# Batch 0 taken in the order q, k, v by halves of the heads, and k and v of two batches laid six tokens to a partition

## The chip, the cores and the metric

The kernel runs on one core of one Trainium2 chip. The metric is device time in microseconds for one launch. In the profile the engines are called PE (TensorE, matrix multiplies), PEld (TensorE's weight loads, which run beside its multiplies), DVE (VectorE), ACT (ScalarE), POOL (GpSimd) and SP (SyncE). SP and POOL issue most of the DMAs here, POOL those that turn f32 in HBM into bf16 in on-chip memory. Each engine works through its own list of instructions in order, and waits at an instruction until what that needs is there.

## The reference: what is computed

Two parts follow each other. The first is a linear attention over 8 batches of 8 heads, 576 tokens and 64 features: q and k are clipped at zero and multiplied by the cosine and by the sine of a position angle, which gives 128 features; then k is summed against v over the tokens.

```
q_p = phi(q, cos_w, sin_w)          # max(x, 0) times cos, beside max(x, 0) times sin: 128 features
k_p = phi(k, cos_w, sin_w)
kv  = einsum('bhsf,bhsd->bhfd', k_p, v)
z   = sum(k_p, axis=2)
num = einsum('bhsf,bhfd->bhsd', q_p, kv)
den = einsum('bhsf,bhf->bhs', q_p, z)[..., None] + 1e-06
x   = (num / den), all heads of a token side by side: 4608 tokens of 512
```

The second part is a feed-forward layer over the 4608 tokens: h = x @ w_in (512 to 2048), g = h * sigmoid(1.702 h), out = g @ w_out (2048 to 512).

## The kernel before

**Layout.** A batch of q, k or v has 576 tokens. The first 512 lie four to a partition on 128 partitions (`load_main`), so that token 4p + c is chunk c of partition p; the last 64 are a tail of their own, one to a partition on 64 partitions (`load_tail`), and are chunk 4. `kp` holds k after the clipping and the two multiplications, five chunks by 8 heads by 128 features; `vt` holds v in bf16 with a 65th column of ones, so that one multiplication gives both kv and z. `qn` is q after the same treatment, and `qT` is `qn` turned so that features lie on the partitions.

**The steps of one batch.** `prep` makes a chunk of `kp` or `qn` (two operations, cosine and sine, L179 on DVE or L177 on ACT). `prep_v` casts a chunk of v into `vt` (L182). `unit_kv` multiplies `kp` with `vt`, 8 heads by five chunks (L213), and copies the result to `kvs` (L217). `turn_q` turns a chunk of q by a DMA transpose (L189), `turn_q_at` by eight matmuls with the identity and a DVE copy (L195, L196). `unit_num` multiplies a chunk of `qT` with `kvs` (L233), and DVE divides (L239 to L241) into `xb`. `turn_x` or `turn_x_at` turns `xb` into `xT` (L206, or L201 and L203).

**The feed-forward layer** goes over nine blocks of 512 tokens. A block has 32 slots: 16 `mm1` (four matmuls of L249 and an ACT activation, L254), then 16 groups of four matmuls of `mm2` (L289). Nothing is scheduled by a planner: the order of every engine's instructions is the order in which the program writes them. The attention of batch i + 1 is written into the slots of block i by `at(slot, function)`: the function comes right after that slot's matmuls. In block 0 the numbers are k0 = 14 (preparing batch 1's q and turning it), k1 = 25 (`unit_kv`), and 26 to 29 for the `unit_num`s.

**The front** is batch 0's own attention, ahead of block 0. PE starts with 34 matmuls on zeros (L68). k comes first, in f32, by one load on SP (L109), then its tail and v's tail on SP; q and v come through POOL. ACT and DVE prepare k together, then DVE prepares q chunk by chunk, `turn_q0` turns each chunk (L331, copied by L332), and v is cast by halves of the heads. kv of heads 0 to 3 is `kv_lo`, of heads 4 to 7 `kv_hi`. `num0(n, p)` multiplies half n of the heads with the pair p of chunks (L338) and lets ACT make the denominator (L342); `product0` divides on DVE (L348, L349); `turn_x0` turns the result (L355, L357). The first three groups of `mm1` are written out by hand in parts (`mm1_first`, L361), as far as `xT` is there. The tail of batch 0's q is prepared last and turned by a DMA transpose into `qT_tail`; `unit_num(0, 4)` uses it in slot 7 of block 0.

**Buffers.** `mm` has four PSUM buffers of one bank, `at` two of two banks: a new use waits for the readers of the use four (or two) before. `qn` has one buffer, q, k and v of later batches two each. POOL has at most eight DMAs under way: the ninth waits until the first has landed.

Of the kernel before, what the change touches and what calls it, by code (L numbers as in the profile page):

```python
# [9 lines left out]
F32 = mybir.dt.float32  # L10
# [11 lines left out]
def kernel(  # L22
# [27 lines left out]

    def rows(c):
        return 128 if c < 4 else 64

    warm = const.tile([128, TB], BF16)
    nc.vector.memset(warm, 0.0)  # L57

    def mm_tile():
        return ps.tile([128, TB], F32, name="mm", bufs=4)  # L60
# [11 lines left out]
    SRC = {"q": q, "k": k, "v": v}  # L72

    def load_main(b, n, h0=0, h1=H, on=nc.gpsimd):
        if h0 == 0:
            state[b][n] = two.tile([128, 2048], BF16, name=n)
        on.dma_start(out=state[b][n][:, 256 * h0:256 * h1].rearrange("p (h e) -> p h e", h=h1 - h0),  # L77
                     in_=SRC[n][b, h0:h1, 0:512, :].rearrange("h (p c) d -> p h (c d)", c=4))
# [23 lines left out]
    def load_w_out(g):  # L102
        nc.gpsimd.dma_start(out=w_out_sb[:, ts(g, 4), :], in_=wout_r[:, ts(g, 4), :])

    pos_i = const.tile([128, NC], I32)
    id_i = const.tile([128, 128], I32)
# [12 lines left out]
    load_w_in(0, 0, 2)  # L119
# [19 lines left out]
    kp = one.tile([128, NC, H, 2 * D], BF16, name="kp")  # L139
    vt = one.tile([128, NC, H, VW], BF16, name="vt")  # L140
    qT = one.tile([128, H, NC * 128], BF16, name="qT")
    nc.vector.memset(kp[64:128, 4], 0.0)
    nc.vector.memset(vt[64:128, 4], 0.0)
    nc.vector.memset(vt[:, 0:4, :, D:D + 1], 1.0)
    nc.vector.memset(vt[0:64, 4, :, D:D + 1], 1.0)
    qT_tail = one.tile([128, H, 128], BF16, name="qT_tail")
    nc.vector.memset(qT[:, :, S:NC * 128], 0.0)
    nc.vector.memset(qT_tail[:, :, 64:128], 0.0)
    pos_f = const.tile([128, NC], F32)
    nc.vector.tensor_copy(pos_f, pos_i)  # L150
    ident = const.tile([128, 128], BF16)
    nc.vector.tensor_scalar(ident, id_i, 0.0, None, op0=EQ)
    sinw = const.tile([128, NC], F32)
    cosw = const.tile([128, NC], F32)
    nc.scalar.activation(sinw, pos_f, AF.Sin, scale=scale)
    nc.scalar.activation(cosw, pos_f, AF.Sin, scale=-scale, bias=halfpi)
    gelu0 = const.tile([128, 1], F32)
    nc.scalar.activation(gelu0, halfpi, AF.Gelu_apprx_sigmoid)

# [1 line left out]


    def part(b, n, c, h0, h1):
        if c == 4:
            return state[b][n, 4].rearrange("p (h d) -> p h d", d=D)[:, h0:h1]
        return state[b][n].rearrange("p (h c d) -> p c h d", c=4, d=D)[:, c, h0:h1]

    def prep_new(b):
        state[b]["qn"] = one.tile([128, NC, H, 2 * D], BF16, name="qn")
# [1 line left out]

    def prep(b, n, c, h0=0, h1=H, on=(nc.vector, nc.vector)):
        o = state[b]["qn"] if n == "q" else kp
        for cs, w in enumerate((cosw, sinw)):
            oc, i, wc = o[:rows(c), c, h0:h1, cs * D:cs * D + D], part(b, n, c, h0, h1), w[:rows(c), c:c + 1]
            if on[cs] is nc.scalar:
                nc.scalar.activation(oc, i, AF.Relu, scale=wc)  # L177
            else:
                nc.vector.tensor_scalar(oc, i, 0.0, wc, op0=MAX, op1=MUL)  # L179

    def prep_v(b, c, h0=0, h1=H):
        nc.vector.tensor_copy(vt[:rows(c), c, h0:h1, 0:D], part(b, "v", c, h0, h1))  # L182

    def q_slot(b, c):

# [22 lines left out]


    def kv_half(b, n, kv):  # L210
        for h in range(4 * n, 4 * n + 4):
            for c in range(NC):
                nc.tensor.matmul(kv[:, ds(h % 4 * (D + 1), D + 1)], kp[:, c, h, :], vt[:, c, h, 0:D + 1],  # L213
                                 start=(c == 0), stop=(c == NC - 1))

    def kvs_half(b, n, kv, copy=nc.vector.tensor_copy):
        copy(state[b]["kvs"][:, n, :, 0:D + 1], kv[:, 0:4 * (D + 1)].rearrange("p (h e) -> p h e", h=4))  # L217

    def kvs_new(b):
        state[b]["kvs"] = two.tile([128, 2, 4, VW], BF16, name="kvs")  # L220
# [102 lines left out]

    prep_new(0)
    s0 = state[0]
    dens = {}

    def turn_q0(c, copy):
        t = mm_tile().bitcast(BF16).rearrange("p (h t) -> p h t", h=H)
        for h in range(H):  # L330
            nc.tensor.transpose(t[:, h], s0["qn"][:, c, h, :], ident)  # L331
        copy(qT[:, :, ts(c, 128)], t)  # L332
# [12 lines left out]
    def product0(n, p):  # L345
        nm4, den = dens[n, p]
        inv = two.tile([128, 2, 4], F32, name="inv")
        nc.vector.reciprocal(inv, den)  # L348
        nc.vector.tensor_tensor(s0["xb"][:, 2 * p:2 * p + 2, 4 * n:4 * n + 4, :], nm4[:, :, :, 0:D],  # L349
                                inv.unsqueeze(3).to_broadcast([128, 2, 4, D]), op=MUL)  # L350
# [12 lines left out]

    AC, VE = nc.scalar, nc.vector
    kvs_new(0)
    warmup(34)
    for c in range(4):
        prep(0, "k", c, on=(VE, AC))
    prep(0, "k", 4)
    for c in range(2):  # L370
        prep(0, "q", c)
        turn_q0(c, AC.copy)
    prep_v(0, 4)
    for c in range(4):
        prep_v(0, c, 0, 4)
    kv_lo = mm_tile()
    kv_half(0, 0, kv_lo)
    kvs_half(0, 0, kv_lo, AC.copy)
    num0(0, 0)
    for c in (2, 3):  # L380
        prep(0, "q", c)
    for c in range(4):
        prep_v(0, c, 4, 8)
    turn_q0(2, AC.copy)
    product0(0, 0)
    turn_q0(3, VE.tensor_copy)
    kv_hi = mm_tile()
    kv_half(0, 1, kv_hi)
    kvs_half(0, 1, kv_hi, AC.copy)
    num0(0, 1)  # L390
    product0(0, 1)
    tp = mm_tile().bitcast(BF16).rearrange("p (q s j t) -> p q s j t", q=2, s=2, j=2)
    first = [mm_tile() for _ in range(3)]
    turn_x0(0, 0)
    num0(1, 0)
    product0(1, 0)
    turn_x0(0, 1)
    num0(1, 1)
    product0(1, 1)
    turn_x0(1, 0)  # L400
    for fc in range(3):
        mm1_first(fc, (0, 1), 0, TB)
    turn_x0(1, 1)
    for p in range(2):
        for fc in range(3):
# [87 lines left out]
```

## Time and profile before

| | us |
|---|---|
| median of 4 runs (lowest to highest) | 300.14 (299.38 to 301.56) |
| the profiled execution | 299.71 |
| span of its instructions | 297.6 |
| PE busy | 286.5 (96%) |
| DVE, ACT, POOL busy | 107.4, 120.6, 92.5 |
| first matmul of L249 in the main loop | 22.46 |
| start of block 1 | 57.0 |
| last matmuls (L313) | 289.76 to 293.26 |

The span is that of the profiled execution, from the first instruction to the last. Its own time is 2.1 us longer, and lies within the range of the runs. A row of the profile has the line of the kernel, the engine, the operation, what it writes and reads, and how often; in the timeline and the chain the first two numbers are start and length in us from the start of the span.

### The profile page before, as it was taken

The numbers are of one execution on the slowest core, as the hardware profiler recorded it, in microseconds if no ns is written. First come the engines' busy times: TensorE is split into PE (matmuls) and PEld (weight loads), VectorE is DVE, ScalarE is ACT, GpSimd is POOL, SyncE is SP. The second block draws the span as 40 slices with busy tenths as digits, with TensorE's granted clock in tenths as the row PEclk, the third lists the DMA queues.
The fourth block names the chain that finished last, engine by engine and source line by source line (L and its number), as shares of the span: only waits on it lengthen the run. The fifth ranks groups of instructions, "written<-read, shape, count | busy, mean of one in ns | idle before, by whom it ended". The sixth has DMA issues, their size and how long they took to land.

```text
span 297.6 us, 5050 instructions
## 1 busy us (share of the span) xinstructions
PE 286.5 (96%) x1956; PEld 144.6 (49%) x1956; DVE 107.4 (36%) x349; ACT 120.6 (41%) x205; POOL 92.5 (31%) x113
## 2 busy tenths in 40 slices
PE   8877999999999999999999999999999999999994
PEld 3563455545544554455445544554455444444443
DVE  3860376781590158115811481148214200000000
ACT  5555600664127412651165116511651176136410
POOL 8442130440269025800690159004401200120021
PEclk9999999999999999999999999999999999999999
DMA  8999999999979955997699789946804500021033
GB/s 193 195 204 194 184 193 195 200 153 151 203 156 182 184 100 128 192 163 136 134 176 178 121 144 192 193 89 134 176 0 64 124 35 2 36 79 27 2 71 71
DMA packets 89847, 39.84 MB, mean 134 GB/s; under 512 B 58656, under 2 KB 87584, under 8 KB 89824
## 3 DMA queue, kind: packets, MB, share of 16 engines
q0 software_dynamic: 41312, 26.68, 59.3%
q1 hardware_dynamic: 48352, 12.72, 24.1%
q8 instruction: 15, 0.25, 0.3%
q10 hardware_dynamic: 160, 0.13, 0.2%
q14 instruction: 8, 0.07, 0.1%
HBM read 36.70 MB, written 9.44 MB: 155 GB/s over the span
## 4 chain that ended last, share of the span: by engine, by line
PE 86%; DVE 6%; DMA 6%; issue 1%; ACT 0%; DVEq 0%; POOLq 0%
PE mm L249 39%; PE mm L289 38%; PE at L233 3%; DMA q<-in_q_dram 3%; PE at L213 3%; DMA qT_tail<-qn 3%; PE mm L313 1%; DVE kp L179 1%; DVE qn L179 1%; DVE xb L349 1%; DVE vt L182 1%; PE at L195 1%; DVE xb L241 1%; DVE qT L196 0%; ACT den L342 0%
## 5 line engine op out<-in xcount | busy, mean ns | idle before, releaser
L289 PE MATMUL mm<-w_out_sb,g 128*128 128x512 bf16 x560 | 129.0, 379 | 0.0
L249 PE MATMUL mm<-xT,w_in_sb 128*128 128x512 bf16 (+1 forms) x568 | 124.6, 377 | 0.0
L254 ACT ACTIVATE g<-mm 128x512 bf16<-128x512 f32 x144 | 85.6, 597 | 48.1 <-PE mm L249 47.5
L301 POOL DMA_DIRECT2D out_dram<-ysb x54 | 50.6, 941 | 173.7 <-ACT ysb L299 173.0
L249 PEld LDWEIGHTS <-w_in_sb 128*128 128x128 bf16 x568 | 54.7, 98 | 64.1 <-issue 0.2
L289 PEld LDWEIGHTS <-g 128*128 128x128 bf16 x560 | 52.1, 98 | 56.5
L299 ACT COPY ysb<-mm 128x512 f32<-128x512 f32 x34 | 19.9, 586 | 112.7 <-PE mm L289 109.4
L217 DVE CAST kvs<-at 128x260 bf16<-128x260 f32 x14 | 5.4, 426 | 56.3 <-PE at L213 56.3
L241 DVE TENSOR_TENSOR xb<-at,inv 128x512 bf16<-128x512 f32 (+1 forms) x36 | 24.8, 689 | 1.2
L239 DVE TENSOR_SCALAR den<-at 128x8 f32<-128x8 f32 (+1 forms) x36 | 5.9, 164 | 53.0 <-PE at L233 53.0
L318 DVE COPY ysb<-mm 128x256 f32<-128x256 f32 x1 | 0.4, 425 | 59.4 <-PE mm L313 59.4
L233 PEld LDWEIGHTS <-qT 128*128 128x128 bf16 x280 | 13.4, 98 | 8.4 <-DVE xb L241 0.6
L233 PE MATMUL at<-kvs,qT 128*128 128x65 bf16 x280 | 14.6, 194 | 0.3
L179 DVE TENSOR_SCALAR kp<-k,cosw 128x512 bf16<-128x512 bf16 (+1 forms) x32 | 12.2, 389 | 3.5 <-DMA k<-in_k_dram 3.5
L213 PEld LDWEIGHTS <-kp 128*128 128x128 bf16 x320 | 11.1, 97 | 2.6 <-ACT qT L332 0.4
L179 DVE TENSOR_SCALAR qn<-q,sinw 128x512 bf16<-128x512 bf16 x32 | 11.5, 361 | 0.0
L179 DVE TENSOR_SCALAR qn<-q,cosw 128x512 bf16<-128x512 bf16 x32 | 11.0, 345 | 0.6 <-DMA q<-in_q_dram 0.6
L68 PE MATMUL mm<-warm 128*128 128x512 bf16 x34 | 9.4, 446 | 1.2 <-DVE warm L57 1.2
L213 PE MATMUL at<-vt,kp 128*128 128x65 bf16 x280 | 10.1, 193 | 0.2
L179 DVE TENSOR_SCALAR kp<-k,sinw 128x512 bf16<-128x512 bf16 x28 | 9.5, 340 | 0.0
L77 POOL DMA_DIRECT2D v<-in_v_dram x9 | 7.9, 883 | 2.0 <-DMA w_out_sb<-in_moe_w_out_dram 2.0
L77 POOL DMA_DIRECT2D q<-in_q_dram x8 | 7.5, 936 | 3.4 <-DMA w_in_sb<-in_moe_w_in_dram 2.0
(67 smaller groups left out, 119.4 us busy)
## 6 DMA issues: line engine op xcount, KB each, us to landing
out_dram<-ysb POOLq DMA_DIRECT2D x38, 128.0 KB, 3.0
q<-in_q_dram POOLq DMA_DIRECT2D x8, 512.0 KB, 9.3
out_dram<-ysb POOLq DMA_DIRECT2D x16, 256.0 KB, 2.7
k<-in_k_dram POOLq DMA_DIRECT2D x7, 512.0 KB, 11.2
v<-in_v_dram POOLq DMA_DIRECT2D x7, 512.0 KB, 12.7
w_out_sb<-in_moe_w_out_dram POOLq DMA_DIRECT2D x4, 512.0 KB, 24.7
w_in_sb<-in_moe_w_in_dram POOLq DMA_DIRECT2D x3, 512.0 KB, 13.8
k<-in_k_dram SPq DMA_DIRECT2D x1, 1024.0 KB, 5.8
```

The source lines that it names most:

```text
L68: nc.tensor.matmul(wps, warm[:, 0:128], warm, start=True, stop=True)
L77: on.dma_start(out=state[b][n][:, 256 * h0:256 * h1].rearrange("p (h e) -> p h e", h=h1 - h0), in_=SRC[n][b, h0:h1, 0:512, :].rearrange("h ...
L179: nc.vector.tensor_scalar(oc, i, 0.0, wc, op0=MAX, op1=MUL)
L213: nc.tensor.matmul(kv[:, ds(h % 4 * (D + 1), D + 1)], kp[:, c, h, :], vt[:, c, h, 0:D + 1], start=(c == 0), stop=(c == NC - 1))
L233: nc.tensor.matmul(nm[:, h // 4, ds(h % 4 * (D + 1), D + 1)], q_slot(b, c)[:, h, :], state[b]["kvs"][:, h // 4, h % 4, 0:D + 1], start=Tru ...
L239: nc.vector.tensor_scalar(den[:r], nm4[:, :, :, D], 1e-6, None, op0=ADD)
L241: nc.vector.tensor_tensor(state[b]["xb"][:r, c].rearrange("p (n h) d -> p n h d", n=2), nm4[:, :, :, 0:D], inv[:r].unsqueeze(3).to_broadca ...
L249: nc.tensor.matmul(hps[:, c0:c1], w_in_sb[:, kc, ds(fc * 128, 128)], xT[:, kc, ds(i * TB + c0, c1 - c0)], start=(kc == 0), stop=(kc == KC ...
L254: nc.scalar.activation(g, hps, AF.Gelu_apprx_sigmoid)
L289: nc.tensor.matmul(yps, gT[fc][:, ds(t * 128, 128)], w_out_sb[:, fc, :], start=(fc == 0), stop=(fc == FC - 1))
L299: nc.scalar.copy(ysb, cur[t])
L301: nc.gpsimd.dma_start(out=out[row:row + (n - 1) * step + 1:step, :], in_=ysb[p0:p0 + n, :])
```

## The change

Batch 0 is taken in the order q, k, v:

- q of batch 0 is what SP loads in f32, in two halves of four heads (`q0`); k goes through POOL in two halves of the heads, ahead of v. The tails of k and v of batch 0 are no longer loaded by themselves.
- k and v of batches 0 and 1 have six tokens to a partition on 96 partitions (`wide`), all 576 tokens in one load, with position tables of their own (`pos6_i`, `cos6`, `sin6`). `kp` and `vt` have six chunks; `unit_kv` of batch 1 goes over six chunks of 96 rows instead of five. Of batch 1 SP loads only q's tail. From batch 2 on the old layout holds, so that the 64 unused rows of chunk 4 of `kp` and `vt` are zeroed in slot 2 of block 1.
- v of batch 0 is not copied to `vt`: `kv0` multiplies `kp` with the loaded tile itself. Each matmul has 128 moving columns, 64 of v and 64 ones from a strip behind it (48 * D to 49 * D).
- `turn_q0(n, p)` turns two chunks of half the heads. Three of the four are done ahead of k. `num0` has its denominator made by DVE, and `product0` is merged into it. 30 warm-up matmuls instead of 34.
- In block 0, `unit_num(0, 4)` goes from slot 7 to 13, k0 from 14 to 11 with all five chunks of q in one slot and their turns in slots 14 to 18, k of batch 1 into slot 18, k1 from 25 to 23, the `unit_num`s to slots 24 to 27.

```diff
     def load_main(b, n, h0=0, h1=H, on=nc.gpsimd):
+        t = 6 if wide(b, n) else 4
+        np_ = 96 if wide(b, n) else 128
...
-    state[0]["k"] = k0 = one.tile([128, 2048], F32, name="k0")
-    nc.sync.dma_start(out=k0.rearrange("p (h e) -> p h e", h=H),
-                      in_=k[0, :, 0:512, :].rearrange("h (p c) d -> p h (c d)", c=4))
-    load_tail(0, "k", nc.sync)
-    load_tail(0, "v", nc.sync)
-    load_main(0, "q")
+    state[0]["q"] = q0 = one.tile([128, 2048], F32, name="q0")
+    for n in range(2):
+        nc.sync.dma_start(out=q0[:, ts(n, 1024)].rearrange("p (h e) -> p h e", h=4),
+                          in_=q[0, 4 * n:4 * n + 4, 0:512, :].rearrange("h (p c) d -> p h (c d)", c=4))
     nc.gpsimd.iota(pos_i[:, 0:4], pattern=[[1, 4]], base=0, channel_multiplier=4)
     nc.gpsimd.iota(pos_i[:, 4:5], pattern=[[1, 1]], base=512, channel_multiplier=1)
+    nc.gpsimd.iota(pos6_i, pattern=[[1, 6]], base=0, channel_multiplier=6)
+    load_main(0, "k", 0, 4)
     nc.gpsimd.iota(id_i, pattern=[[1, 128]], base=0, channel_multiplier=-1)
+    load_main(0, "k", 4, 8)
     load_main(0, "v", 0, 4)
     load_main(0, "v", 4, 8)
...
     def kv_half(b, n, kv):
+        r, last = (96, 5) if b < 2 else (128, 4)
         for h in range(4 * n, 4 * n + 4):
-            for c in range(NC):
-                nc.tensor.matmul(kv[:, ds(h % 4 * (D + 1), D + 1)], kp[:, c, h, :], vt[:, c, h, 0:D + 1],
-                                 start=(c == 0), stop=(c == NC - 1))
+            for c in range(last + 1):
+                nc.tensor.matmul(kv[:, ds(h % 4 * (D + 1), D + 1)], kp[:r, c, h, :], vt[:r, c, h, 0:D + 1],
+                                 start=(c == 0), stop=(c == last))
...
+    def turn_q0(n, p, copy):
+        t = mm_tile().bitcast(BF16).rearrange("p (h s t) -> p h s t", h=4, s=2)
+        for h in range(4):
+            for s in range(2):
+                nc.tensor.transpose(t[:, h, s], s0["qn"][:, 2 * p + s, 4 * n + h, :], ident)
+        copy(qT[:, 4 * n:4 * n + 4, ds(256 * p, 256)].rearrange("p h (s t) -> p h s t", s=2), t)
+
+    def kv0(n):
+
+        kv = mm_tile()
+        v3 = s0["v"][:96].rearrange("p (j d) -> p j d", d=D)
+        for h in range(4):
+            for c in range(6):
+                j = (4 * n + h) * 6 + c
+                nc.tensor.matmul(kv[:, ts(h, 128)].rearrange("p (j d) -> p j d", j=2), kp[:96, c, 4 * n + h, :],
+                                 v3[:, j:49:48 - j, :], start=(c == 0), stop=(c == 5))
+        kvs_half(0, n, kv, nc.scalar.copy, 128)
...
-        nc.scalar.activation(den, nm4[:, :, :, D], AF.Identity, bias=eps)
-        dens[n, p] = nm4, den
-
-    def product0(n, p):
-        nm4, den = dens[n, p]
         inv = two.tile([128, 2, 4], F32, name="inv")
+        nc.vector.tensor_scalar(den, nm4[:, :, :, D], 1e-6, None, op0=ADD)
         nc.vector.reciprocal(inv, den)
...
-    warmup(34)
...
+    warmup(30)
+
+    def prep_q0(n, p):
+        for c in (2 * p, 2 * p + 1):
+            prep(0, "q", c, 4 * n, 4 * n + 4)
+
+    for n, p in ((0, 0), (0, 1), (1, 0)):
+        prep_q0(n, p)
+        turn_q0(n, p, AC.copy)
+    for c in range(6):
+        prep(0, "k", c, 0, 4)
+    prep_q0(1, 1)
+    for c in range(6):
+        prep(0, "k", c, 4, 8, on=(VE, AC))
+    kv0(0)
+    turn_q0(1, 1, AC.copy)
     num0(0, 0)
...
     num0(0, 1)
-    product0(0, 1)
+    kv0(1)
     tp = mm_tile().bitcast(BF16).rearrange("p (q s j t) -> p q s j t", q=2, s=2, j=2)
     first = [mm_tile() for _ in range(3)]
     turn_x0(0, 0)
     num0(1, 0)
-    product0(1, 0)
     turn_x0(0, 1)
     num0(1, 1)
-    product0(1, 1)
-    turn_x0(1, 0)
     for fc in range(3):
         mm1_first(fc, (0, 1), 0, TB)
+        if fc == 0:
+            turn_x0(1, 0)
     turn_x0(1, 1)
...
-    for n in "kvq":
-        load_tail(1, n, nc.sync)
+    load_tail(1, "q", nc.sync)
...
             if i == 0:
-                at(7, unit_num, 0, 4)
-                at(7, turn_x, 0, 4)
-            k0, k1, ks = (14, 25, (26, 27, 28, 29)) if i == 0 else (0, 12, (17, 19, 21, 23, 25))
+                at(13, unit_num, 0, 4)
+                at(13, turn_x, 0, 4)
+            k0, k1, ks = (11, 23, (24, 25, 26, 27)) if i == 0 else (0, 12, (17, 19, 21, 23, 25))
             at(k0, prep_new, b)
+            if i == 1:
+
+                at(2, nc.vector.memset, kp[64:128, 4], 0.0)
+                at(2, nc.vector.memset, vt[64:128, 4], 0.0)
             for c in range(NC):
-                at(22 if i == 0 and c == 4 else k0, prep, b, "q", c)
+                at(k0, prep, b, "q", c)
                 if i == 0:
-                    at(23 if c == 4 else k0 + 2 + c, turn_q_at, b, c)
+                    at(k0 + 3 + c, turn_q_at, b, c)
                 else:
                     at(k0 + c, turn_q, b, c)
-                at(k1 - 4 + c // 2, prep, b, "k", c)
+            for c in range(6 if b < 2 else NC):
+                at(18 if i == 0 else k1 - 4 + c // 2, prep, b, "k", c)
                 at(k1 - 1, prep_v, b, c)
             at(k1, unit_kv, b)
```

More of the change, by code (lines that the diff above doesn't have):

```diff
@@ L54, in rows, with wide, krows @@
         return 128 if c < 4 else 64
+    def wide(b, n):
+        return b < 2 and n != "q"
+    def krows(b, c):
+        return 96 if b < 2 else rows(c)
     warm = const.tile([128, TB], BF16)
@@ L74, in load_main @@
     def load_main(b, n, h0=0, h1=H, on=nc.gpsimd):
+        t = 6 if wide(b, n) else 4
+        np_ = 96 if wide(b, n) else 128
         if h0 == 0:
-            state[b][n] = two.tile([128, 2048], BF16, name=n)
-        on.dma_start(out=state[b][n][:, 256 * h0:256 * h1].rearrange("p (h e) -> p h e", h=h1 - h0),
-                     in_=SRC[n][b, h0:h1, 0:512, :].rearrange("h (p c) d -> p h (c d)", c=4))
+            state[b][n] = two.tile([128, 2048 if n == "q" else 49 * D], BF16, name=n)
+        on.dma_start(out=state[b][n][:np_, t * D * h0:t * D * h1].rearrange("p (h e) -> p h e", h=h1 - h0),
+                     in_=SRC[n][b, h0:h1, 0:np_ * t, :].rearrange("h (p c) d -> p h (c d)", c=t))
     def load_tail(b, n, on=nc.gpsimd):
@@ L105 @@
     pos_i = const.tile([128, NC], I32)
+    pos6_i = const.tile([128, 6], I32)
     id_i = const.tile([128, 128], I32)
-    state[0]["k"] = k0 = one.tile([128, 2048], F32, name="k0")
-    nc.sync.dma_start(out=k0.rearrange("p (h e) -> p h e", h=H),
-                      in_=k[0, :, 0:512, :].rearrange("h (p c) d -> p h (c d)", c=4))
-    load_tail(0, "k", nc.sync)
-    load_tail(0, "v", nc.sync)
-    load_main(0, "q")
+    state[0]["q"] = q0 = one.tile([128, 2048], F32, name="q0")
+    for n in range(2):
+        nc.sync.dma_start(out=q0[:, ts(n, 1024)].rearrange("p (h e) -> p h e", h=4),
+                          in_=q[0, 4 * n:4 * n + 4, 0:512, :].rearrange("h (p c) d -> p h (c d)", c=4))
     nc.gpsimd.iota(pos_i[:, 0:4], pattern=[[1, 4]], base=0, channel_multiplier=4)
     nc.gpsimd.iota(pos_i[:, 4:5], pattern=[[1, 1]], base=512, channel_multiplier=1)
+    nc.gpsimd.iota(pos6_i, pattern=[[1, 6]], base=0, channel_multiplier=6)
+    load_main(0, "k", 0, 4)
     nc.gpsimd.iota(id_i, pattern=[[1, 128]], base=0, channel_multiplier=-1)
+    load_main(0, "k", 4, 8)
     load_main(0, "v", 0, 4)
@@ L138, with table @@
     nc.vector.memset(eps, 1e-6)
-    kp = one.tile([128, NC, H, 2 * D], BF16, name="kp")
-    vt = one.tile([128, NC, H, VW], BF16, name="vt")
+    pos_f = const.tile([128, NC], F32)
+    nc.vector.tensor_copy(pos_f, pos_i)
+    pos6_f = const.tile([128, 6], F32)
+    nc.vector.tensor_copy(pos6_f, pos6_i)
+    ident = const.tile([128, 128], BF16)
+    nc.vector.tensor_scalar(ident, id_i, 0.0, None, op0=EQ)
+    kp = one.tile([128, 6, H, 2 * D], BF16, name="kp")
+    vt = one.tile([128, 6, H, VW], BF16, name="vt")
     qT = one.tile([128, H, NC * 128], BF16, name="qT")
[L142 to L145, printed above, removed]
     qT_tail = one.tile([128, H, 128], BF16, name="qT_tail")
+    nc.vector.memset(state[0]["v"][:, 48 * D:49 * D], 1.0)
+    nc.vector.memset(vt[:, :, :, D:D + 1], 1.0)
     nc.vector.memset(qT[:, :, S:NC * 128], 0.0)
     nc.vector.memset(qT_tail[:, :, 64:128], 0.0)
[L149 to L156, printed above, removed]
+    def table(name, shape, pos, bias, sign):
+        t = const.tile(shape, F32, name=name)
+        nc.scalar.activation(t, pos, AF.Sin, scale=sign * scale, bias=bias)
+        return t
+    cosw = table("cosw", [128, NC], pos_f, halfpi, -1.0)
+    sinw = table("sinw", [128, NC], pos_f, 0.0, 1.0)
+    cos6 = table("cos6", [128, 6], pos6_f, halfpi, -1.0)
+    sin6 = table("sin6", [128, 6], pos6_f, 0.0, 1.0)
     gelu0 = const.tile([128, 1], F32)
@@ L163, in part @@
     def part(b, n, c, h0, h1):
+        if wide(b, n):
+            return state[b][n][:96, 0:48 * D].rearrange("p (h c d) -> p c h d", c=6, d=D)[:, c, h0:h1]
         if c == 4:
             return state[b][n, 4].rearrange("p (h d) -> p h d", d=D)[:, h0:h1]
-        return state[b][n].rearrange("p (h c d) -> p c h d", c=4, d=D)[:, c, h0:h1]
+        return state[b][n][:, 0:32 * D].rearrange("p (h c d) -> p c h d", c=4, d=D)[:, c, h0:h1]
     def prep_new(b):
@@ L173, in prep @@
         o = state[b]["qn"] if n == "q" else kp
-        for cs, w in enumerate((cosw, sinw)):
-            oc, i, wc = o[:rows(c), c, h0:h1, cs * D:cs * D + D], part(b, n, c, h0, h1), w[:rows(c), c:c + 1]
+        r = rows(c) if n == "q" else krows(b, c)
+        for cs, w in enumerate((cos6, sin6) if wide(b, n) else (cosw, sinw)):
+            oc, i, wc = o[:r, c, h0:h1, cs * D:cs * D + D], part(b, n, c, h0, h1), w[:r, c:c + 1]
             if on[cs] is nc.scalar:
@@ L181, in prep_v @@
     def prep_v(b, c, h0=0, h1=H):
-        nc.vector.tensor_copy(vt[:rows(c), c, h0:h1, 0:D], part(b, "v", c, h0, h1))
+        nc.vector.tensor_copy(vt[:krows(b, c), c, h0:h1, 0:D], part(b, "v", c, h0, h1))
     def q_slot(b, c):
@@ L210, in kv_half, with kvs_half @@
     def kv_half(b, n, kv):
+        r, last = (96, 5) if b < 2 else (128, 4)
         for h in range(4 * n, 4 * n + 4):
-            for c in range(NC):
-                nc.tensor.matmul(kv[:, ds(h % 4 * (D + 1), D + 1)], kp[:, c, h, :], vt[:, c, h, 0:D + 1],
-                                 start=(c == 0), stop=(c == NC - 1))
-    def kvs_half(b, n, kv, copy=nc.vector.tensor_copy):
-        copy(state[b]["kvs"][:, n, :, 0:D + 1], kv[:, 0:4 * (D + 1)].rearrange("p (h e) -> p h e", h=4))
+            for c in range(last + 1):
+                nc.tensor.matmul(kv[:, ds(h % 4 * (D + 1), D + 1)], kp[:r, c, h, :], vt[:r, c, h, 0:D + 1],
+                                 start=(c == 0), stop=(c == last))
+    def kvs_half(b, n, kv, copy=nc.vector.tensor_copy, w=D + 1):
+        copy(state[b]["kvs"][:, n, :, 0:D + 1],
+             kv[:, 0:4 * w].rearrange("p (h e) -> p h e", h=4)[:, :, 0:D + 1])
     def kvs_new(b):
@@ L325 @@
     s0 = state[0]
[L326 to L332, printed above, removed]
+    nums = {}
+    def turn_q0(n, p, copy):
[13 more added lines that the diff above has]
+        kvs_half(0, n, kv, nc.scalar.copy, 128)
     def num0(n, p):
@@ L365 @@
     kvs_new(0)
-    warmup(34)
[L367 to L378, printed above, removed]
-    num0(0, 0)
[L380 to L389, printed above, removed]
+    warmup(30)
[12 more added lines that the diff above has]
+    turn_q0(1, 1, AC.copy)
+    num0(0, 0)
     num0(0, 1)
-    product0(0, 1)
+    kv0(1)
     tp = mm_tile().bitcast(BF16).rearrange("p (q s j t) -> p q s j t", q=2, s=2, j=2)
```

## The prediction

> **What bounds the kernel now.** I read the engine totals first, then the stretches of busy time, the chain of work that ended last, PE's waits in the first block, and then the timeline of the first 57 us.
>
> ```profile
> PE 286.5 (96%) x1956; PEld 144.6 (49%) x1956; DVE 107.4 (36%) x349; ACT 120.6 (41%) x205; POOL 92.5 (31%) x113
> ...
> 57.00:265.00 208.00, 208.00 (x1388) 102.55 (x1386) 76.61 (x256) 83.27 (x140) 68.63 (x74) 1.00 0.82 132
> ```
>
> The second line is a stretch, with PE's busy time first: from 57.0 us, where block 1 starts, PE never stops. What the change does can therefore show only in when block 1 starts. That has two parts: the front (batch 0's attention, until the first main-loop matmul of L249 at 22.46 us) and block 0 (from there to 57.0).
>
> ```profile
> 13.64 0.39 ACT kvs L217
> ...
> 19.70 0.69 DVE xb L349
> 20.39 0.66 DVE qn L179 x2
> 21.04 0.02 issue
> 21.06 7.73 DMA qT_tail<-qn
> 28.79 0.05 issue
> 28.84 0.43 PE at L233 x8
> 29.26 6.91 PE mm L249 x32
> ...
> 45.18 0.42 PE at L195 x8
> ...
> 46.83 1.15 DVE vt L182 x5
> 47.98 0.04 issue
> 48.02 1.24 PE at L213 x36
> ```
>
> This is the chain, with start and length. PE is full but for stalls: unit_num(0,4) waits for the DMA transpose of q's tail, then the last turn of batch 1's q waits for DVE, then kv of batch 1 waits for the copies of v. PE's waits give the first its size:
>
> ```profile
> PE at L233 <- DMA qT_tail<-qn: 1.9, 1, 1.9
> PE at L195 <- DVE qn L179: 0.3, 1, 0.3
> ```
>
> In the timeline the kv matmuls begin at 47.25 and go on in earnest at 48.02: 0.77 more. The L233 groups of chunks 2 and 3 begin at 52.75 and 54.40, each 0.31 after PE came free. Stalls of block 0: 1.89 + 0.31 + 0.77 + 0.62 = 3.6 us.
>
> **The front, step by step.** Before, its last part is kvs_hi (ACT, ends 16.40), then four rounds of num0 and product0 on DVE, the last L361 matmuls, and L249 at 22.46. The new order makes ACT the engine that is late. The rows:
>
> ```profile
> 1.19 9.39 PE L68 MATMUL mm<-warm 128*128 128x512 bf16 x34 [1.19 <-DVE warm L57]
> 6.60 2.56 ACT L177 ACTIVATE kp<-k,sinw 128x512 bf16<-128x512 f32 x4 [1.71 <-DMA k<-in_k_dram]
> 11.68 1.93 ACT L332 COPY qT<-mm 128x1024 bf16<-128x1024 bf16 x2 [2.52 <-PE mm L331]
> ```
>
> - Warm-up: from 5.0 us its matmuls start 0.215 apart; four fewer end it 0.86 earlier, near 9.7. The transposes of q follow in order; eight take 0.45, so ACT's first copy starts at 10.2.
> - q must be there by then. The 1 MB of k on SP landed at 0.74 + 5.8 = 6.5; the same bytes are now q's two halves, estimated at 5.0 and 6.4. Twelve DVE multiplies of 256 f32 elements at about 0.3 (half of 0.585, the spacing of four of 512 in 2.34) end near 8.7. POOL's two added halves of k, one added iota and the iotas now ahead of the loads delay its first load by about 0.4, but its queue moved only 0.03 MB before 6 us while SP's load ran, so nothing is lost. At 0.2 MB/us after that, k lands by halves near 8.3 and 9.7, v near 11.2 and 12.7.
> - ACT, in order: three copies of 1024 columns (0.92 apart, 1.01 alone: 2.85), until 13.05. Then six multiplies of k's high half by the sine, 256 columns each. [...] The row has 0.707 us for 512 columns and 0.617 from one to the next; scaled by the columns alone, six would take 1.85. [...] ACT reaches kvs of the low half at 15.4 (0.38): 15.75.
> - kv0 of the low half is 24 matmuls of 128 moving columns, 0.056 each as in the transposes: 1.35. Even if it waits for all of v it ends near 14.1, and the turn of q's last quarter follows: hidden behind ACT. So the omitted casts of v (1.5 us of DVE) and the memsets buy nothing here; DVE is free from 12.8.
> - num0(0,0): 0.45 on PE. Then DVE makes den (0.21), inv (0.23) and the product (0.69), 1.13 a round by L239 to L241's spacing; taking den over from ACT costs DVE 0.2 and saves a hop. kv0 of the high half sits behind two num0s on PE (16.5 to 17.85), its kvs copy ends at 18.3, and round three starts at 18.75, 0.25 after round two ended. Round four ends at 21.0, against 20.4 before.
> - Transpose (0.25), ACT copy (0.6), last six matmuls (0.65), with 0.3 between: L249 starts at 22.8. **Front: +0.35.** Bounds: -0.2 with ACT's six by columns, +1.0 if v's high half is 2 us later than estimated.
>
> **Block 0.**
> - unit_num(0,4) moves from slot 7 to 13, which begins eleven matmul groups of 0.863 (29.26 6.91 x32: 0.216 each) after 22.8, at 32.3. The tail's transpose starts near 21.7 and with 7.73 lands at 29.45. **-1.89**, hidden by six more groups of mm1; cover left 2.9.
> - Now all of batch 1's q is prepared at slot 11, ahead of that unit's den on DVE. The new qn has one buffer, so it waits for the same transpose: 29.45, eight operations of 0.26: 31.55. The fifth chunk needs the tail of q, loaded by SP right behind the transpose. kt and vt of batch 1 are gone from that queue:
>
> ```profile
> kt<-in_k_dram SPq DMA_DIRECT2D x1, 128.0 KB, 8.9
> qt<-in_q_dram SPq DMA_DIRECT2D x1, 128.0 KB, 13.8
> ...
> q0 software_dynamic: 237, 0.12, 87.8%
> q1 hardware_dynamic: 237, 0.06, 45.8%
> ```
>
> The first two lines are issue to landing: 22.41 + 8.9 = 31.3 and 23.73 + 13.8 = 37.5. The last two are packets and MB in the microsecond from 31: the queues take turns packet by packet, and SP's 512 packets of 256 bytes take 2.1 us at 240 per us, 3.2 at 160. So q's tail lands at 31.6 to 32.7; I take 32.0, since kt in the same place took 2.5. DVE ends it at 32.8, and the tail unit's three operations at 33.9, before the second turn wants its PSUM buffer at 34.8. No stall; the earlier 0.31 goes.
> - k and v of batch 1: six chunks where there were five. Turns end on PE at 39.1, the last copy on DVE at 39.55; twelve multiplies at 0.26 end at 42.8, six casts (0.20 apart) at 44.05. PE reaches kv at 43.4 and loses 0.5 where it lost 0.77: **-0.27**. Eight more matmuls (1.21 / 40 each): **+0.24**. The product stalls (0.62) stay.
> - Transfers: w_out's second quarter landed at 15.79 + 24.3 = 40.1 (wanted at 39.9), v of batch 1 at 16.54 + 26.2 = 42.7 (wanted at 42.8), w_out's third quarter at 45.3 (wanted at 45.3). All would be just in time even unmoved. Without kt and vt POOL's queue runs at 0.2 and not 0.13 MB/us for about 5 us (0.35 MB, 1.8 us), less 0.13 MB of tails that it now carries (0.7): about 1 us earlier. **0.**
> - The two memsets of kp and vt in block 1 (0.76) lie in DVE's idle time before slot 8: 0; without cover they'd cost that.
>
> Sum: +0.35 - 1.89 - 0.31 - 0.27 + 0.24 = -1.9. The span goes from 297.6 to 295.7, the profiled execution from 299.71 to 297.8, and the median from 300.14 to **298.2**.
>
> **Rivals.**
> - *The gain is eaten in the front* (0.14; about 299.5). PE is loaded unevenly from 11 to 19 us. [...] Warm-up shows both speeds (0.43 and 0.215 apart), and the stall of 1.9 at 27 us left no slow matmul. [...] ACT or DVE slower by 1.3 us ends in the same place.
> - *q's tail holds DVE* (0.12; slower). It is queued on DVE in front of the tail unit and of every turn's copy, which free PE's buffers. Past about 32.9 each us of lateness costs PE one; at 34.8 the gain is gone. At the old 37.5, DVE is done with the tail unit at 39.4, PE waits from 34.8, and 4.6 - 1.9 gives 302.8. Against it: two loads of 512 packets left that queue.
> - *96 partitions load slower than 128* (0.08). If four such loads (2.36 MB, 12 us at 0.2 MB/us) ran at three quarters, v lands 4 us later less 1, its casts end at 47.1, kv stalls 3.7 for 0.5: 301.3. No row shows such a load.
> - *ACT's short operations scale, and DVE's rounds close up* (0.12): 297.2.
>
> **How the numbers follow.** Measurement tells about 0.5% (1.5 us) from no change. The sum as it stands has 0.54, with its own range 297.3 to 299.1, of which 0.46 lies under 298.6. Faster: 0.46 + 0.12 = 0.58; same: 0.08 + 0.14 = 0.22; slower: 0.12 + 0.08 = 0.20. The range runs from 296.6, the front at -0.2 with DVE's 0.5 at kv gone too and 0.6 for the rounding of a dozen terms, to 301.5, past the slow-load case; the late tail's far end stays outside.
>
> **What would show it.** The kvs copy of the low half near 15.4 on ACT, right behind six short multiplies; L249 near 22.8; no wait of L233 for qT_tail; L213 in block 0 near 43.9 behind DVE; block 1 near 55.1; no gap after. Wrong if PE stands at the first turns of batch 1's q while DVE waits for a DMA, if kv waits for v's load, or if matmuls in L361 start 0.43 apart.

## The result

The changed kernel takes 297.13 us (median of 30 runs, 296.37 to 301.91), the kernel before 299.84 (49 runs, 299.06 to 302.12). The ratio is 0.9915, with a 95% interval of 0.9899 to 0.9931: 0.85% faster, 2.5 us (2.7 between the medians). The forecast was 298.2, 1.9 us faster.

In some executions of either kernel PE's mean clock is lower: 0.982 to 0.994 in 17 of 42 of the changed kernel, with a median of 299.08 where the other 25 have 296.86 (the profiled one, 299.08 with a span of 297.3, is of the 17, at 0.993), and 0.989 to 0.996 in 26 of 81 of the kernel before, of which 16 took 301.25 or more where the other 55 have a median of 299.64.

First the chain of work that ended last, of the changed kernel, with start and length in us. The lines of before have moved: L238 is the old L217 (kvs), L271 the old L249, L255 the old L233, L215 the old L195, L234 the old L213.

```profile
10.78 2.84 ACT qT L355 x3
13.62 2.37 ACT kp L197 x6
15.99 0.27 ACT kvs L238
16.26 0.04 issue
16.31 0.97 PE at L372 x16
17.28 2.57 PE mm L364 x24
...
25.25 9.50 PE mm L271 x44
34.74 0.25 PE at L255 x8
35.00 0.86 PE mm L271 x4
35.86 0.45 PE at L215 x8
...
46.31 1.46 PE at L234 x43
```

Two things are to be seen. In block 0 the tail unit (L255) follows its slot's matmuls without a gap, and so do the first turns (L215); no DMA stands on the chain any more where it had 7.7 us. In the front ACT's six sines stand before kvs, as foretold, and PE waits behind them. The 24 matmuls of L364 take 2.57 us, though (2.75 by the timeline, where the low half's 24, at 11.79, take 1.50 at a clock of 1.00).

PE's row in the timeline has the length of that wait in brackets; the stretches of the same profile have the granted clock as the third number from the end (after PE, PEld, DVE, ACT and POOL):

```profile
16.31 0.97 PE L372 MATMUL at<-kvs,qT 128*128 128x65 bf16 x16 [2.57 <-ACT kvs L238]
```

```profile
10.00:15.00 5.00, 3.58 (x58) 3.20 (x57) 4.16 (x18) 4.22 (x7) 3.17 (x4) 1.00 1.32 192
15.00:20.00 5.00, 3.69 (x44) 3.69 (x44) 2.03 (x6) 2.28 (x6) 2.73 (x4) 0.66 1.27 206
20.00:25.00 5.00, 4.30 (x49) 2.99 (x47) 2.67 (x8) 2.65 (x6) 0.80 (x1) 1.00 1.34 202
```

PE waited 2.57 us, until 16.31, and the clock was 0.66 in the stretch from 15 to 20. By the timeline the main loop then starts at 25.08 us and block 1 at 57.07, no earlier than before (22.46 and 56.85). The run of the changed kernel below has a profile at full clock.

### The profile page after: what moved, and what is told of

Same layout as the page of the kernel before. It is cut to its first block, busy times and chain, and to the rows that moved or that the text cites. A ratio compares the mean times of both kernels' runs of the same rounds, so it can differ in the third digit from the quotient of the medians.

```text
span 297.3 us, 5091 instructions
## 1 busy us (share of the span) xinstructions
PE 288.5 (97%) x1968; PEld 147.4 (50%) x1968; DVE 109.6 (37%) x367; ACT 120.6 (41%) x206; POOL 93.0 (31%) x115
## 4 chain that ended last, share of the span: by engine, by line
PE 95%; ACT 2%; DVE 1%; issue 0%; DVEq 0%
PE mm L271 41%; PE mm L311 40%; PE at L255 3%; PE at L234 3%; PE mm L75 3%; PE mm L335 1%; PE mm L391 1%; ACT qT L355 1%; PE mm L364 1%; ACT kp L197 1%; PE at L215 1%; DVE xb L263 1%; ACT xT L387 0%; PE at L372 0%; PE mm L385 0%
## 5 line engine op out<-in xcount | busy, mean ns | idle before, releaser
L271 PE MATMUL mm<-xT,w_in_sb 128*128 128x512 bf16 (+1 forms) x568 | 124.7, 378 | 0.0
L271 PEld LDWEIGHTS <-w_in_sb 128*128 128x128 bf16 x568 | 54.7, 98 | 64.1
L238 DVE CAST kvs<-at 128x260 bf16<-128x260 f32 x14 | 5.4, 426 | 55.6 <-PE at L234 55.6
L255 PEld LDWEIGHTS <-qT 128*128 128x128 bf16 x280 | 13.4, 98 | 8.4 <-DVE xb L263 0.6
L199 DVE TENSOR_SCALAR qn<-q,cosw 128x512 bf16<-128x512 bf16 (+1 forms) x36 | 12.2, 340 | 9.5 <-DMA qT_tail<-qn 8.5
L255 PE MATMUL at<-kvs,qT 128*128 128x65 bf16 x280 | 14.6, 194 | 0.3
L199 DVE TENSOR_SCALAR qn<-q,sinw 128x512 bf16<-128x512 bf16 (+1 forms) x36 | 13.6, 377 | 0.0
L234 PEld LDWEIGHTS <-kp 128*128 128x128 bf16 (+1 forms) x288 | 9.8, 97 | 1.9
L234 PE MATMUL at<-vt,kp 128*128 128x65 bf16 (+1 forms) x288 | 10.3, 193 | 0.0
L86 POOL DMA_DIRECT2D k<-in_k_dram x9 | 7.8, 865 | 3.7 <-ACT g L276 2.8
L223 ACT COPY xT<-at 128x512 bf16<-128x512 bf16 x4 | 2.4, 588 | 14.4 <-PE at L221 14.4
L199 DVE TENSOR_SCALAR kp<-k,cosw 128x512 bf16<-128x512 bf16 x24 | 8.1, 339 | 0.0
## 6 DMA issues: line engine op xcount, KB each, us to landing
k<-in_k_dram POOLq DMA_DIRECT2D x6, 512.0 KB, 11.8
```

The costliest lines, as they stand in the source:

```text
L86: on.dma_start(out=state[b][n][:np_, t * D * h0:t * D * h1].rearrange("p (h e) -> p h e", h=h1 - h0), in_=SRC[n][b, h0:h1, 0:np_ * t, :].r ...
L234: nc.tensor.matmul(kv[:, ds(h % 4 * (D + 1), D + 1)], kp[:r, c, h, :], vt[:r, c, h, 0:D + 1], start=(c == 0), stop=(c == last))
L255: nc.tensor.matmul(nm[:, h // 4, ds(h % 4 * (D + 1), D + 1)], q_slot(b, c)[:, h, :], state[b]["kvs"][:, h // 4, h % 4, 0:D + 1], start=Tru ...
L271: nc.tensor.matmul(hps[:, c0:c1], w_in_sb[:, kc, ds(fc * 128, 128)], xT[:, kc, ds(i * TB + c0, c1 - c0)], start=(kc == 0), stop=(kc == KC ...
```

## The experiments

The clock counts below are executions with a mean clock under 0.997. Ratios are to the kernel before, run on the same chip, with 95% intervals.

### The changed kernel again

No edit.

> The changed kernel once more, for a second profile. The first profiled execution took 299.08 us against a median of 297.13 over its runs, and its 24 matmuls of kv0 of the high half took 2.75 us where full speed needs 1.35. Theory (PE's clock falls to half after the 2.6 us in which PE waits for the low half's kvs copy, in some executions only): a profile with full clock shows these matmuls at 1.35 us, L271 starting near 22.9 instead of 25.08, block 1 near 55.0 and a span near 295.3; the ratio stays 0.9915. Rival (the front is always that slow and block 0 gave more than the prediction said): L271 starts at 25 us again, with a span near 297.

Measured: 297.44 us, ratio 0.9926 (0.9896 to 0.9956); the profiled execution took 297.25 (span 295.5). ACT's part of the front in its timeline, the stretch from 15 us, and PE's waits in the front:

```profile
9.74 2.84 ACT L355 COPY qT<-mm 128x1024 bf16<-128x1024 bf16 x3 [5.51 <-PE mm L354]
12.46 2.51 ACT L197 ACTIVATE kp<-k,sin 96x256 bf16<-96x256 bf16 x6
14.86 0.37 ACT L238 CAST kvs<-mm 128x260 bf16<-128x260 f32 x1
```

```profile
15.00:20.00 5.00, 3.99 (x71) 3.44 (x71) 3.69 (x12) 2.58 (x5) 3.07 (x4) 1.00 1.28 206
```

```profile
12.13 1.50 PE L364 MATMUL mm<-v,kp 96*128 96x128 bf16 x24 [1.53 <-DMA v<-in_v_dram]
...
15.28 0.67 PE L372 MATMUL at<-kvs,qT 128*128 128x65 bf16 x16 [1.20 <-ACT kvs L238]
```

At full clock the matmuls of L364 take 1.50 us by the timeline (2.75 in the first profile, by the same view), L271 starts at 22.52 and block 1 at 55.23. So the first theory holds, but for a part: of the 2.56 us by which L271 was later in the first profile, the clock took some 1.5 (1.25 in L364, and 0.3 in L372, which took 0.97 there and 0.67 here). The other 1.0 was lost before the wait: the warm-up took 9.10 us there and some 8.06 here (ended 0.48 before ACT's first copy there, and taken so here), and that copy started at 10.78 and not at 9.74.

Here PE waits twice in the front, 1.53 for v and then 1.20 for kvs. In the first profile, where the warm-up ended later, it waited 0.15 for v and then 2.57 at once. Two more profiles of kernels with this front fit: waits of 1.4 and 1.3 at a clock of 1.00 (24 warm-up matmuls, below), and of 0.5 and 2.3 with a clock of 0.57 from 15 to 20 us (the tail unit back in slot 7, below). This suggests that a late warm-up decides which executions lose the clock; four profiles don't show it.

Block 0 is longer here than there (32.7 us against 32.0), which the chain explains: DVE was released in slot 11 by the main load of batch 1's q, landed at 30.4, and PE lost 0.6 us at the second turn, behind the tail unit's operations on DVE.

```profile
12.28 18.12 DMA q<-in_q_dram
...
30.89 3.19 DVE qn L199 x10
```

```profile
PE at L215 <- DVE xb L263: 0.6, 1, 0.6
```

### The tail unit alone in slot 13, in the kernel before

```diff
-                at(7, unit_num, 0, 4)
-                at(7, turn_x, 0, 4)
+                at(13, unit_num, 0, 4)
+                at(13, turn_x, 0, 4)
```

> The kernel before with one edit: unit_num(0, 4) and its turn_x in slot 13 instead of 7. If the stall of 1.89 us for qT_tail is all that this edit touches: -1.9 us (ratio 0.994). Theory of just-in-time transfers: w_out's third quarter landed at 45.3 us in the profile of before, and slot 24 used it at 45.5; with PE 1.9 us ahead, slot 24 waits for it about 1.5 us, so that only 0.3 to 0.5 us is left (ratio 0.998 to 0.999).

Measured: 297.55 us, ratio 0.9928 (0.9900 to 0.9955), clock low in 0 of 7. Two lines moved give 2.3 of the 2.7 us between the medians, with the old front and the old loads. The theory of just-in-time transfers failed. PE's waits in block 0:

```profile
PE at L195 <- DVE qn L179: 0.2, 1, 0.2
PE mm L289 <- DMA w_out_sb<-in_moe_w_out_dram: 0.2, 1, 0.2
```

It waited 0.2 us for w_out, and not 1.5, because the transfers came earlier too. The load of batch 1's k took 23.2 us from issue to landing in the profile of before; here, and in the next two runs, which have the same move, it took 20.8, 20.5 and 21.6:

```profile
k<-in_k_dram POOLq DMA_DIRECT2D x1, 512.0 KB, 20.8
```

`turn_x` of the tail, a DMA transpose, went with its unit from 30.4 to 34.1 us, so that only the last 1.7 us of that load run beside it. That this is what made the load shorter isn't shown: no run moves `turn_x` by itself.

### All slot numbers of the change, in the kernel before

The front and the loads are those of before; slots 13, 11, 18, 23 and 24 to 27 are those of the change. Two of the lines:

```diff
-            k0, k1, ks = (14, 25, (26, 27, 28, 29)) if i == 0 else (0, 12, (17, 19, 21, 23, 25))
+            k0, k1, ks = (11, 23, (24, 25, 26, 27)) if i == 0 else (0, 12, (17, 19, 21, 23, 25))
...
-                at(22 if i == 0 and c == 4 else k0, prep, b, "q", c)
+                at(k0, prep, b, "q", c)
```

> The kernel before, with its front and its loads, and all slot numbers of block 0 from the change (13 for the tail unit, 11 for batch 1's q, 18 for its k, 23 for kv, 24 to 27 for the unit_nums). Rival of the prediction, the late tail of q: SP loads it third, it landed at 37.5 us, DVE is held there, the second turn of batch 1's q waits from 34.4 to 39.4: 2 us slower than before (ratio 1.007). If the queue position of q's tail does not matter: 2 us faster (0.993).

Measured: 304.25 us, ratio 1.0134 (1.0108 to 1.0160), clock low in 6 of 6. The prediction's slower rival is real where q's tail is third on SP. PE's wait, and the chain:

```profile
PE at L195 <- DVE xb L241: 4.8, 1, 4.8
```

```profile
24.05 13.72 DMA qt<-in_q_dram
37.77 0.02 issue
37.80 0.87 DVE qn L179 x2
...
39.75 1.03 PE at L195 x8
40.78 1.71 PE mm L289 x4
42.49 0.85 PE at L195 x8
43.34 1.71 PE mm L289 x4
45.05 0.60 PE at L195 x8
45.65 0.86 PE mm L289 x4
```

q's tail landed at 37.8, DVE went on, and PE, which had waited 4.8 us (4.6 to 5.0 were foretold), came back at half speed: 1.71 us for four matmuls that take 0.86, until 45 us. Counting what these lines take over 0.45 and 0.86, the clock cost 0.58 + 0.85 + 0.40 + 0.85 + 0.15 = 2.8 us. That covers the 2.4 us between the 4.4 measured and the 2 expected.

### The same, with q's tail first on SP

```diff
-    for n in "kvq":
+    for n in "qkv":
         load_tail(1, n, nc.sync)
```

> As the run before (old front, new slot numbers), with SP loading batch 1's tails in the order q, k, v instead of k, v, q. If the position of q's tail is what decides, it lands near 31.5 us and nothing holds DVE: -2.1 us against the kernel before (ratio 0.993), with kv waiting 0.9 us for v's casts behind v's load at 42.7. If instead the change's larger loads (six tokens to a partition, no tails of k and v) are needed to have v and w_out in time, PE waits for them in slots 20 to 24: -0.5 us or less (0.998).

Measured: 298.36 us, ratio 0.9933 (0.9908 to 0.9959). One letter's place in a string is worth 5.9 us against the run before. The stall is gone (PE's only wait over 0.15 us from 20 to 60 us is 0.4 for a copy in the front). So the late tail was only a matter of what SP loads first, and the larger loads of the change aren't needed to avoid it. By the medians (298.36, and 297.55 with the tail unit alone) the other slot moves add nothing to the tail unit's; the intervals overlap.

### The tail unit back in slot 7, in the changed kernel

```diff
-                at(13, unit_num, 0, 4)
-                at(13, turn_x, 0, 4)
+                at(7, unit_num, 0, 4)
+                at(7, turn_x, 0, 4)
```

> The changed kernel with unit_num(0, 4) and its turn_x back in slot 7, all else as changed. Theory (this move is nearly the whole gain): q's tail lands near 29.1 us and slot 7 ends near 26.9, so PE stands 2.2 us there; 0.6 of it comes back, because the first turns of batch 1's q then no longer wait. 1.6 to 2.2 us slower than the changed kernel: ratio 0.998 to 1.000 to the kernel before. Rival (the new front and layout carry the gain): the ratio stays at 0.993 or below.

Measured: 300.90 us, ratio 1.0020 (1.0000 to 1.0041), clock low in 8 of 12; the four at full clock have a median of 299.21, 2.35 more than the changed kernel's 296.86. Without the one move nothing of the gain is left in the median, and 0.4 us at full clock. Together with the run of the move alone this shows the cause from both sides.

The stall itself is not in this run's profile, whose mean clock was 0.983: PE's clock was 0.57 from 15 to 20 us and 0.50 from 20 to 25, L271 started at 26.91, and the transpose had landed (23.4 + 7.7 = 31.1) just before slot 7's unit, which didn't wait:

```profile
31.23 0.42 PE L255 MATMUL at<-kvs,qT_tail 128*128 128x65 bf16 x8
```

### ACT's sines to DVE, in the changed kernel

```diff
-        prep(0, "k", c, 4, 8, on=(VE, AC))
+        prep(0, "k", c, 4, 8)
```

> The changed kernel with the sines of k's high half made by DVE instead of ACT. Theory (ACT is the late engine of the front): the low half's kvs copy comes at about 13.6 us instead of 14.9, DVE's first division about 0.9 us earlier, L271 starts near 21.5 instead of 22.5. Whole: if the front decides, -1.0 us against the changed kernel (ratio 0.989); if the load of batch 1's q, which landed at 30.4 us and released DVE in slot 11, decides block 0, the first turns of q wait 1 us longer and the time is the changed kernel's (0.992).

Measured: 295.91 us, ratio 0.9859 (0.9816 to 0.9902), clock low in 0 of 4. PE's part of the front in the timeline:

```profile
13.26 0.61 PE L354 MATMUL mm<-ident,qn 128*128 128x128 bf16 x8
14.12 0.67 PE L372 MATMUL at<-kvs,qT 128*128 128x65 bf16 x16 [0.25 <-ACT kvs L238]
14.62 0.61 PE L364 MATMUL mm<-v,kp 96*128 96x128 bf16 x5
15.67 1.23 PE L364 MATMUL mm<-v,kp 96*128 96x128 bf16 x19 [0.43 <-DVE den L377]
...
22.14 2.11 PE L271 MATMUL mm<-xT,w_in_sb 128*128 128x512 bf16 x9
```

The wait before L372 fell from 1.2 (in the second profile above) to 0.25, and the time by 1.0 us against the changed kernel at full clock. ACT was the late engine of the front. L271 starts only 0.4 earlier than there, because ACT's first copy started 1.2 us later in this profile (10.94 against 9.74), behind a longer warm-up; from that copy to L271 it is 11.2 us, where it was 12.8. Block 0 didn't give the gain back to q's load: PE waits for nothing there, and block 0 takes 32.0 us.

### Fewer warm-up matmuls, in the changed kernel

```diff
-    warmup(30)
+    warmup(24)
```

> The changed kernel with 24 warm-up matmuls instead of 30. Theory: the end of the warm-up releases ACT's copies, and so the front: 6 x 0.215 = 1.3 us earlier at full clock, less what q's third quarter on DVE (ready at 8.4) holds back; L271 near 21.5. In the whole 0 to -1.0 us, by the same two cases as with the sines on DVE. If the clock falls more often, the executions near 299 us become more than 4 in 10.

Measured: 296.24 us, ratio 0.9875 (0.9836 to 0.9914), clock low in 1 of 5: 0.6 us less than the changed kernel at full clock. That lies in the range that was expected and doesn't tell its two cases apart; the profiled execution (297.41) has a wait of 1.0 us at one of the first turns.

### v cast by DVE again, in the changed kernel

```diff
+    for c in range(6):
+        prep_v(0, c, 0, 4)
     for c in range(6):
         prep(0, "k", c, 4, 8, on=(VE, AC))
+    for c in range(6):
+        prep_v(0, c, 4, 8)
...
-        v3 = s0["v"][:96].rearrange("p (j d) -> p j d", d=D)
...
+        kv_half(0, n, kv)
+        kvs_half(0, n, kv, nc.scalar.copy)
```

> The changed kernel with v of batch 0 cast into vt by DVE again (six casts of the low half after the last q, six of the high half after the last k) and multiplied from there with 65 columns. Theory (v as loaded buys nothing, DVE is free and ACT is late): L271 within 0.3 us of 22.5 and the same time. Rival (the casts were on the path): 1 to 1.5 us slower, since the low half's kv starts a us later than ACT is ready for it.

Measured: 298.20 us, ratio 0.9937 (0.9917 to 0.9957), clock low in 11 of 12. Neither side's reason holds. The kvs copy of the low half still starts at 15.07 on ACT (14.86 with v as loaded), so the casts weren't on that path; but PE now stands twice, and the clock falls:

```profile
PE mm L234 <- DVE vt L202: 2.0, 1, 2.0
PE at L367 <- ACT kvs L238: 0.8, 1, 0.8
```

```profile
15.00:20.00 5.00, 4.41 (x64) 4.02 (x64) 4.02 (x15) 2.74 (x6) 2.81 (x4) 0.50 1.30 206
20.00:25.00 5.00, 4.57 (x30) 2.96 (x31) 1.58 (x6) 2.47 (x6) 0.92 (x2) 0.84 1.33 201
```

The median is 1.1 us above the changed kernel's 297.13, so multiplying v as loaded is worth about that. How much of it is the clock isn't shown: the only execution at full clock took 297.96, 1.1 above the changed kernel's 296.86.

### Filler for PE, in the changed kernel

```diff
     turn_q0(1, 1, AC.copy)
+    fill = at_tile()
+    for _ in range(8):
+        nc.tensor.matmul(fill[:, 0], warm[:, 0:128], warm, start=True, stop=True)
     num0(0, 0)
```

> The changed kernel with eight matmuls on zeros on PE behind the turn of q's last quarter, where PE waits for the low half's kvs copy; nothing reads their result. Theory (that wait lets PE's clock fall in some executions): no execution with a mean clock near 0.992 and none near 299 us; the executions at full clock are unmoved at 297. Rival (the clock falls for another reason): the same share of executions, about 4 in 10, near 299 us.

Measured: 298.20 us, ratio 0.9949 (0.9928 to 0.9970), clock low in 0 of 17, against 17 of 42 without filler. So the wait before L372 is where the clock is lost. The second half of the theory failed: at full clock the filled kernel is 1.3 us slower than the changed one. Its profile (299.71 us) has 1.4 us of waiting at a turn of batch 1's q, whose tail landed at 22.2 + 11.8 = 34.0, and another 1.4 in block 1 for a DMA transpose:

```profile
PE at L215 <- DVE xb L263: 1.4, 1, 1.4
```

```profile
PE at L255 <- DMA qT<-qn: 1.4, 1, 1.4
```

The second wait isn't the filler's doing alone: the next run, without filler, has such waits too. Why the filled kernel is slower stays open.

### Sines to DVE and fewer warm-up matmuls together

The edits of both runs.

> Sines of k's high half on DVE and 24 warm-up matmuls together. Each alone gave about 1.0 and 0.7 us against the changed kernel at full clock. If both shorten one chain through ACT: the low half's kvs then waits for v's load (11.8) and its matmuls, and DVE for its own twelve multiplies until 14.9, so that only 0 to 0.4 us is added to the sines' 1.0: 295.6 us, ratio 0.986. If they were independent: 295.2, ratio 0.985.

Measured: 296.00 us, ratio 0.9891 (0.9851 to 0.9930), clock low in 0 of 6: no better than the sines alone. The two shorten one chain; in this profile PE waits 2.8 us for v's load instead. The profiled execution took 299.89, the others 295.64 to 296.73. What sets it apart comes later, in block 1, where a transpose of q took 11.2 us to land:

```profile
PE at L255 <- DMA qT<-qn: 2.6, 2, 1.4
```

### The last chunk of batch 1's q in slot 16

```diff
-                at(k0, prep, b, "q", c)
+                at(16 if i == 0 and c == 4 else k0, prep, b, "q", c)
```

On top of the run before, and then with 30 warm-up matmuls again.

> As the run before, with the fifth chunk of batch 1's q (the only one that needs SP's late tail) prepared in slot 16 instead of 11, behind the tail unit and the first turns on DVE. Theory (that tail holds DVE in front of the turns, 4.8 us in the run with it third on SP, 1.4 in the run with the filler): the stalls of the first turns that it causes go; 0.2 to 0.8 us faster than the run before, and a narrower spread. Rival (batch 1's main load of q, landing at 29 to 30.6, is the last to come): no difference.

> The best single edit (sines of k's high half on DVE, 30 warm-up matmuls, 295.9 us) with the fifth chunk of batch 1's q prepared in slot 16. Theory: with 30 warm-up matmuls PE waits less before kv0 (0.5 us there against 2.5 to 2.8 with 24), so the clock stays full in all executions; the late tail can't hold DVE in slot 11; 295.5 to 295.9 us, ratio 0.986 to 0.987. If the tail of q mattered in no execution of that kernel, it is the same 295.9.

Measured: 296.62 us, ratio 0.9894 (0.9869 to 0.9918), clock low in 4 of 6, its two at full clock at 296.0 and 296.2; and with 30, 296.17 us, ratio 0.9859 (0.9824 to 0.9895), clock low in 0 of 6. Neither beats the kernel that it was put on. In the profiles of those two kernels no first turn waited anyway, so the theory gets no support. The sines on DVE, with or without this, make the fastest kernel here: 1.4% faster than before, and about 0.9 us ahead of the changed kernel at full clock.

## Why the prediction was right, and where its sizes were off

- **The tail unit, -1.89.** Right, and most of the gain by itself: moved alone it gives 2.3 us between the medians, and moving it back costs 2.35 at full clock. Its transpose landed at 29.1 in the second profile (29.45 was said) and was used at 32.0. With the unit in slot 13 and the old front none of 19 executions was slowed by the clock (the run of this move alone and the one with q's tail first on SP), where 16 of 81 of the kernel before were. So part of the mean gain may be that the stall no longer lets the clock fall; no profile has such an execution.
- **The front, +0.35: this term was mis-sized.** Its path was right. The sum's 15.4 for kvs has 2.4 us for the six sines, a term that no row of the kernel before shows; its row scaled by the columns gives 1.85, and the changed kernel's profiles showed 2.40 (12.46 to 14.86) and 2.37 (13.62 to 15.99). From ACT's first copy to L271 it is 12.8 us (22.52 - 9.74), where the sum had 12.6. What was off is the front that it was compared with. The profile of before had L249 at 22.46, but in the three later profiles with that front it starts at 22.9 to 23.0, with DVE taking up q at 10.85 (tail unit alone) instead of 10.35. By these the term was about -0.45 (22.52 less 22.97), 0.8 from the forecast, and the new front is no loss. It rests on one profile against three, and ACT's first copy alone came 1.0 apart in two profiles of the changed kernel; the 0.7 us between the tail unit alone (297.55) and the changed kernel at full clock (296.86) agrees. One aside failed: that the omitted casts of v buy nothing. With the casts the kernel was 1.1 us slower; how much of that is the clock stays open.
- **The first turns, -0.31 and no new stall.** Right in the first profile, where PE came there 2.6 us later, and not in the second, which has a stall of 0.6. The sum checked the two SP transfers in front of slot 11, the transpose and q's tail, and left out POOL's main load of q, which landed at 30.4: DVE began at 30.9 and not at 29.45. PE at the first turns while DVE waits for a DMA is a sign of being wrong that the prediction itself named; it came, at a small size.
- **kv, -0.27 + 0.24.** Right: in the chain above the last casts hold L234 from 45.86 to 46.31 (0.45, where 0.5 was said and 0.77 was lost before), and the other 43 of kv's 48 matmuls take 1.46.
- **Transfers, 0.** Right for PE. k of batch 1 took 20.2 us from issue to landing, so it landed 2.8 us earlier; about 1 was said, for the tails taken off SP's queue. In the second profile it took 20.7 and landed 1.9 earlier. Most of it needs no other loads: with the old ones and only the tail unit moved k is already 1.8 earlier. The transpose that moved along may be the reason; the sum left it out.
- **The rivals.** The late tail was well sized as a stall (4.6 said, 4.8 measured) when its condition was made true, and undersized as a time, since the clock's fall behind it, 2.8 us by the chain, was left out. The gain eaten in the front had a part of 0.14, at about 299.5: 17 of 42 executions came there, with a low clock and a median of 299.08, 2.2 us above the others; in the one profiled PE had waited 2.57 us, and the clock was 0.66 from 15 to 20 us. From what wait on the clock falls, no run shows. The 96-partition loads ran no slower: 576 KB in 20.2 and 20.7 us, where 512 KB took 23.2 before and 20.5 to 21.6 with the tail unit moved.
- **The sum.** That it came so near was partly luck: the front was 0.8 better than said, and the first turns 0.9 worse (0.6 of stall, where 0.31 was to go). Between the profiles of before and of the changed kernel at full clock block 1 comes 1.6 us earlier (56.85 to 55.23). Some 0.4 more lies behind the last matmul (4.3 us to the end of the span before, 3.9 after). That leaves some 0.7 of the 2.7 between the medians which the two profiles don't show.

## What to carry to other kernels

When a unit waits for a long DMA transpose, first move that unit later in the engine's order; here two lines gave 2.3 of the 2.7 us for which a new layout, a new load order and new slot numbers were written. Before a block of vector work is moved ahead of the copies that free PSUM, order the queue so that its last operand comes first: the same slots were 0.7% faster or 1.3% slower by which tail SP loaded first. And look at who is late in a stage (ACT here): six short operations moved to another engine were worth 1 us.

## What the runs showed of the hardware

- Behind a wait of 4.8 us PE ran at half speed for 5 us in the run with the slots alone (1.71 us for four matmuls that take 0.86, until 45 us), and all its 6 executions had a low clock (0.985 to 0.994). PE's clock also fell to 0.66 in a stretch with a single wait of 2.57 (the changed kernel, 15 to 20 us), to 0.57 and then 0.50 with one of 2.3 (the tail unit back in slot 7), and to 0.50 with waits of 2.0 and 0.8 us and 1.8 us of short matmuls between (v cast by DVE). But the two runs with the sines on DVE and 24 warm-up matmuls waited 2.8 and 2.5 us in their profiles at a clock of 1.00. What decides among waits of 2 to 3 us the runs don't settle; only that filling the wait ended it (a low clock in 0 of 17 executions, against 17 of 42).
- The transpose of q's tail (64 rows of 1024 bf16) takes 7.7 to 8.6 us from SP's issue to landing in all 14 profiles, in which the DMAs move 200 to 202 GB/s from 20 to 25 us. Of the later transposes the median is 3.0 (`xT`) to 3.7 (`qT`) in the profile of before, in which they move 132 GB/s from 57 to 265 us.
